# One core: a fixed TensorE order of four long runs per unit in place of planned, interleaved matmuls

## The chip, the cores and the metric

The kernel runs on one core of a Trainium2 chip. The metric is the device time of one execution in microseconds (us). Engine names as in the profile: PE is TensorE, PEld its weight loads, DVE is VectorE, ACT is ScalarE, POOL is GpSimd, SP is the engine that issues most DMAs.

## The reference

Three networks follow each other: windowed attention (4 batches, 8 heads, 576 positions), a gated feed-forward network on 2304 tokens of width 512, and a mixture over 8 experts, the "second network" here. Only the last is touched by the change:

```python
logits = x @ w_gate                          # 2304 x 8
P = np.exp(logits - logits.max())
for _ in range(8):                           # row and column scaling in turn
    P /= P.sum(1, keepdims=True) + 1e-09
    P /= P.sum(0, keepdims=True) + 1e-09
    P *= N / E
for e in range(8):
    h = np.maximum(x @ w1[e], 0.0)           # 2304 x 512 @ 512 x 1024
    out += P[:, e:e + 1] * (h @ w2[e])       # 2304 x 1024 @ 1024 x 512
```

## The kernel before

Every float32 operand is split into a high and a low part, and a product is made of three matmuls (high by high, high by low, low by high).

The second network is cut into 48 units: three groups of 768 tokens, and in each group 16 half experts (512 of an expert's 1024 hidden columns). Odd groups go through the half experts backwards, so the weights at a group's border are kept.

**First matrix of a unit, `gemm1`.** `x @ w1` is made with seven block products in place of eight (a Strassen-like scheme). The sums of weight blocks (s1 to s4) and of token blocks (t1 to t4) are formed ahead. A block product for one of two tiles q of 128 hidden columns is six matmuls of 384 columns (`product`, line 696). Each q has three PSUM banks, pa, pb and pc, and they are used several times in a unit: pa takes a11·b11, is copied by ACT (`p1`, line 720), takes s2·t2 on top, is copied again (`pq`, line 725), then s1·t1 (copied to `u4`, line 732) and at last s4·b22. pb takes s3·t3 and later a22·t4, but only after DVE has read it for the sum `u4` (line 733). pc takes a12·b21. Each of the four results is put through a relu by ACT (line 708) and split by DVE (line 709) into a tile `hh[u, f, t]`, with f from 0 to 3 the hidden tile and t the half of 384 tokens.

**Second matrix, `gemm2`.** For each of six tiles j of 128 tokens, twelve matmuls of 512 columns (line 753) go into one of two banks `py`, and DVE adds the result, scaled by P, to `acc[j]` (line 774; in a group's first half expert ACT writes it). j = 0 to 2 read the `hh` tiles with t = 0, j = 3 to 5 those with t = 1.

**Side work.** `moe2_weights` loads, sums and splits the next half expert (raw `w1r` and `st_w` by SP's DMAs, sums by POOL, high casts by ACT, low parts by DVE and POOL). `x_load` and `x_split` do the same for the next group's tokens. `side` is the routing: the last gating block `gate(5)` (four steps of DMA `sx`, cast, POOL subtraction at line 451 and two matmuls at line 454; all three tiles of a step share three slots of the pool `stg`), a maximum over partitions on POOL (line 662), and eight rounds of row and column scaling on DVE, each with one matmul with `ones` (line 680) for the column sums.

**Order.** The program text runs unit u's `gemm1` and lets `gemm2` of unit u - 1 and the side work advance at its `yield`s. On PE, ACT, DVE and POOL a planner, which simulates the kernel, then orders the instructions by readiness and priority; the text's order is only a priority. So PE's queue mixes the matmuls of lines 696 and 753 in pieces as small as one. Within an engine's queue the order is fixed once built.

Of the kernel before, what the change touches and what calls it, by code (L numbers as in the profile page):

```python
# [8 lines left out]
F32 = mybir.dt.float32  # L9
F32R = mybir.dt.float32r  # L10
AF = mybir.ActivationFunctionType
ALU = mybir.AluOpType
# [5 lines left out]
P = 128  # L18
# [14 lines left out]
def attention_moe_kernel(  # L33
# [14 lines left out]
    nc = tc.nc  # L48
# [361 lines left out]
    GT, TH = 768, 384  # L410
# [21 lines left out]
    def x_split(g):  # L432
        for m in ("b11", "t3", "t2", "b21", "t1", "t4", "b22"):
            for k in range(2):
                src = xsum[g, k][m]
                w = wr.tile([P, 2, 512], F32R, tag="w", name=f"x_{g}_{m}_{k}")
                nc.scalar.copy(w[:, 0, :TH], src)
                nc.vector.tensor_tensor(out=w[:, 1, :TH], in0=src, in1=w[:, 0, :TH].bitcast(F32), op=ALU.subtract)
                xc[m, k] = w
            yield  # L440
# [161 lines left out]
    def run(g):  # L602
        for _ in g:
            pass
# [45 lines left out]
    acp = ctx.enter_context(tc.tile_pool(name="acp", bufs=1, reuse_waits="tile"))  # L650
    rawp = ctx.enter_context(tc.tile_pool(name="rawp", bufs=2, reuse_waits="tile"))
# [40 lines left out]
    def product(ps, a, b, ch, q, first):  # L692
        k = 0
        for kt in range(2):
            for s, t in PASSES:
                nc.tensor.matmul(  # L696
                    ps[:, :TH],
                    lhsT=w1s[ch, a, kt][:, s, q * P : q * P + P],
                    rhs=xc[b, kt][:, t, :TH],
                    start=first and k == 0,  # L700
                    stop=k == 5,
                    skip_group_check=True,
                )
                k += 1
# [6 lines left out]
        )  # L711
        hh[u, f, t] = h

    def gemm1(u, ch):
        for q in range(2):
            pool, tag = ((ps_mm, "mm"), (ps_a, "a"))[q]
            pa, pb, pc = (pool.tile([P, 512], F32, tag=tag, name=f"p{n}_{u}_{q}") for n in "abc")
            p1, pq, u4 = (acp.tile([P, TH], F32, tag=n, name=f"{n}_{u}_{q}", bufs=2) for n in ("p1", "pq", "u4"))
            product(pa, "a11", "b11", ch, q, True)
            nc.scalar.copy(p1, pa[:, :TH])  # L720
            yield 0
            product(pb, "s3", "t3", ch, q, True)
            yield 1
            product(pa, "s2", "t2", ch, q, False)
            nc.scalar.copy(pq, pa[:, :TH])  # L725
            yield 0
            product(pc, "a12", "b21", ch, q, True)
            nc.vector.tensor_tensor(out=p1, in0=pc[:, :TH], in1=p1, op=ALU.add)
            relu_split(u, q, 0, p1)
            yield 1  # L730
            product(pa, "s1", "t1", ch, q, False)
            nc.scalar.copy(u4, pa[:, :TH])
            nc.vector.tensor_tensor(out=u4, in0=pb[:, :TH], in1=u4, op=ALU.add)
            relu_split(u, 2 + q, 1, u4)
            yield 1
            product(pb, "a22", "t4", ch, q, False)
            nc.vector.tensor_tensor(out=pq, in0=pb[:, :TH], in1=pq, op=ALU.add)  # L737
            relu_split(u, 2 + q, 0, pq)
            yield 0
            product(pa, "s4", "b22", ch, q, False)  # L740
            relu_split(u, q, 1, pa[:, :TH])
            yield 0

    def gemm2(u, g, i, ch, last):
        e = ch // 2
        for j in range(GT // P):
            tt = g * (GT // P) + j
            th, jj = divmod(j, TH // P)
            ps = ps_o.tile([P, 512], F32, tag="o", name=f"py_{u}_{j}")
            k = 0  # L750
            for f in range(4):
                for a, bb in PASSES:
                    nc.tensor.matmul(  # L753
                        ps,
                        lhsT=hh[u, f, th][:, a, jj * P : jj * P + P],
                        rhs=w2s[ch, f][:, bb, :],
                        start=k == 0,
                        stop=k == 11,
                    )
                    k += 1  # L760
            if i == 0:
                acc[j] = acp.tile([P, DM], F32, tag=f"acc{j}", name=f"acc_{tt}")
                if g == 0:
                    nc.scalar.copy(acc[j], ps)
                else:
                    nc.scalar.activation(acc[j], ps, AF.Copy, scale=Pm[:, tt, e : e + 1])
            elif g == 0 and i == 1:
                nc.vector.tensor_tensor(out=acc[j], in0=ps, in1=acc[j], op=ALU.add)
            else:
                if g == 0 and i == 2:  # L770
                    nc.gpsimd.tensor_scalar(
                        out=acc[j], in0=acc[j], scalar1=Pm[:, tt, 0:1], scalar2=1.0, op0=ALU.mult, op1=ALU.mult
                    )
                nc.vector.scalar_tensor_tensor(  # L774
                    out=acc[j], in0=ps, scalar=Pm[:, tt, e : e + 1], in1=acc[j], op0=ALU.mult, op1=ALU.add
                )
            if last:
                nc.sync.dma_start(out[tt * P : tt * P + P, :], acc[j])
            yield


    units = []
# [1 line left out]
        chs = list(range(16)) if g % 2 == 0 else list(range(15, -1, -1))  # L784
        units += [(g, i, ch) for i, ch in enumerate(chs)]
    sgen = side()
    for u in range(len(units) + 1):
        g2 = iter(())
        if u > 0:
            pg, pi, pch = units[u - 1]  # L790
            g2 = gemm2(u - 1, pg, pi, pch, pi == 15)
        if u == len(units):
            run(g2)
            break
        g, i, ch = units[u]
        if u == 3:
            run(sgen)
        others = [sgen] if u else []
        if u + 1 < len(units) and units[u + 1][2] != ch:
            others.append(moe2_weights(units[u + 1][2], rawp))  # L800
        if i == 15 and u + 1 < len(units):
            others.append(x_load(g + 1))
        if i == 0 and u > 0:
            xs = x_split(g)
            next(xs, None)
            for _ in g2:
                next(xs, None)
                next(xs, None)
            run(xs)

        def step():
            for o in others:
                next(o, None)

        for more in gemm1(u, ch):
            step()
            if more:
                next(g2, None)
                step()
        run(g2)  # L820
        for o in others:
            if o is not sgen:
                run(o)


# [83 lines left out]
```

## Time and profile before

| | us |
|---|---|
| three runs: median (lowest to highest) | 2155.91 (2154.08 to 2159.35) |
| profiled execution: its time | 2154.89 |
| profiled execution: span of the trace | 2153.1 |
| span in the second network's units, about | 619 to 2150 |

The span is the time from the first to the last instruction on record; some 1.8 us lie around it. A matmul's recorded length goes on after the next one has begun, since matmuls are pipelined; the distance between two starts is what counts. The view "chain in order of time" gives such distances, merged over neighbours that write the same kind of tile.

### The profile page before, as it was taken

How to read it: one execution, taken by the hardware profiler on the slowest of the kernel's cores; microseconds unless marked ns; L12 is line 12 of the kernel's file. 1: busy time of each engine (PE TensorE's matmuls, PEld its weight loads, DVE VectorE, ACT ScalarE, POOL GpSimd, SP SyncE). 2: the span in 40 equal slices, each digit the busy share in tenths (PEclk: the TensorE clock that was granted, in tenths of full speed). 3: DMA queues.
4: the chain of work that ended last, by engine and by line, in shares of the span. 5: the costliest groups of instructions: out<-in, count | busy, mean ns of one | idle time of the engine just before them, and what ended most of it. 6: DMA issues, size and time to landing. Idle time of an engine off the chain costs nothing.

```text
span 2153.1 us, 32685 instructions
## 1 busy us (share of the span) xinstructions
PE 2085.3 (97%) x12546; PEld 1901.9 (88%) x12546; DVE 1227.0 (57%) x2119; ACT 891.6 (41%) x1914; POOL 778.3 (36%) x853
## 2 busy tenths in 40 slices
PE   4799999999998999999999999999999999999999
PEld 3788999999988789899899989989998898999897
DVE  6987323323166766566656556665656566566553
ACT  4565443334245334334434443443434444434431
POOL 3765222112255424334413433433333333333320
PEclk8899999999999999999999999999999999999999
DMA  9233221202132212122212211221222122122110
GB/s 269 77 122 107 73 71 56 70 26 74 43 117 84 69 59 79 54 65 79 69 59 88 79 54 64 79 71 55 71 88 75 53 79 79 52 67 79 60 40 35
DMA packets 83388, 160.90 MB, mean 75 GB/s; under 512 B 10528, under 2 KB 18336, under 8 KB 83232
## 3 DMA queue, kind: packets, MB, share of 16 engines
q1 hardware_dynamic: 76128, 140.63, 20.6%
q10 hardware_dynamic: 7104, 18.19, 3.0%
q8 instruction: 98, 1.61, 0.3%
q14 instruction: 58, 0.48, 0.1%
HBM read 149.34 MB, written 9.44 MB: 74 GB/s over the span
## 4 chain that ended last, share of the span: by engine, by line
PE 87%; DVE 5%; DMA 3%; ACT 2%; issue 2%; POOL 1%; SPq 1%; ACTq 0%; POOLq 0%; DVEq 0%
PE py L753 37%; PE pa L696 18%; PE pb L696 9%; PE po L346 6%; PE pg L372 5%; PE pv L372 5%; PE pc L696 5%; PE psX L183 1%; PE psS L139 1%; DMA sd_v<-in_w_val 1%; DMA st_w<-in_w 0%; DMA vbd<-in_vt 0%; DVE w L505 0%; DVE m_o L270 0%; DMA first<-in_kt 0%
## 5 line engine op out<-in xcount | busy, mean ns | idle before, releaser
L753 PE MATMUL py<-w,h 128*128 128x512 f32 x3456 | 862.1, 393 | 0.6 <-DVE acc L774 0.6
L753 PEld LDWEIGHTS py<-w,h 128*128 128x128 f32 x3456 | 644.8, 188 | 118.7 <-DVE acc L774 1.0
L522 POOL TENSOR_TENSOR w<-st_w,w 128x512 fp32r<-128x512 f32 x184 | 242.2, 1335 | 347.5 <-ACT w L521 338.8
L774 DVE SCALAR_TENSOR_TENSOR acc<-py,Pm,acc 128x512 f32<-128x512 f32 x264 | 194.2, 748 | 277.9 <-PE py L753 277.3
L696 PE MATMUL pa<-x_b,w 128*128 128x384 f32 x1152 | 253.7, 337 | 7.9 <-ACT w L504 7.0
L491 POOL TENSOR_TENSOR w1s<-w1r 128x256 f32<-128x256 f32 x92 | 74.8, 813 | 505.3 <-DVE w L505 504.4
L696 PE MATMUL pa<-x_t,w 128*128 128x384 f32 x1152 | 244.9, 337 | 0.0
L696 PEld LDWEIGHTS pa<-x_b,w 128*128 128x128 f32 x1152 | 206.6, 188 | 19.3 <-ACT w L504 8.2
L696 PEld LDWEIGHTS pa<-x_t,w 128*128 128x128 f32 x1152 | 206.8, 188 | 14.5 <-ACT pq L725 0.3
L372 PE MATMUL pv<-xn,w_v 128*128 128x320 f32 (+1 forms) x1152 | 184.0, 302 | 7.2 <-ACT w_v L283 3.5
L521 ACT CAST w<-st_w 128x512 fp32r<-128x512 f32 x184 | 108.6, 621 | 186.6 <-PE pa L696 85.5
L346 PE MATMUL po<-h,w_o 128*128 128x320 f32 (+1 forms) x1152 | 179.1, 301 | 6.9 <-ACT partial L355 2.7
L372 PE MATMUL pg<-xn,w_g 128*128 128x320 f32 (+1 forms) x1152 | 182.5, 301 | 2.8 <-DVE hf L385 2.6
L372 PEld LDWEIGHTS pv<-xn,w_v 128*128 128x128 f32 x1152 | 164.8, 192 | 12.0 <-ACT w_v L283 4.1
L346 PEld LDWEIGHTS po<-h,w_o 128*128 128x128 f32 x1152 | 161.5, 190 | 12.6 <-DVE partial L357 3.5
L372 PEld LDWEIGHTS pg<-xn,w_g 128*128 128x128 f32 x1152 | 165.0, 193 | 7.1 <-DVE hf L385 3.4
L387 POOL TENSOR_TENSOR h<-hf,h 128x256 fp32r<-128x256 f32 (+1 forms) x96 | 80.7, 843 | 227.1 <-ACT h L386 227.1
L505 DVE TENSOR_TENSOR w<-w1s,w 128x512 fp32r<-128x512 f32 x184 | 124.5, 701 | 22.8 <-ACT w L504 20.6
L504 ACT CAST w<-w1s 128x512 fp32r<-128x512 f32 x184 | 111.3, 620 | 54.8 <-PE pc L696 17.7
L505 DVE TENSOR_TENSOR w<-w1r,w 128x512 fp32r<-128x512 f32 x92 | 110.5, 1201 | 36.6 <-ACT w L504 36.6
L708 ACT ACTIVATE h<-pq 128x384 fp32r<-128x384 f32 x96 | 50.3, 524 | 184.6 <-DVE pq L737 184.4
L696 PE MATMUL pb<-x_t,w 128*128 128x384 f32 x576 | 125.3, 336 | 0.0
(154 smaller groups left out, 2703.7 us busy)
## 6 DMA issues: line engine op xcount, KB each, us to landing
st_w<-in_w SPq DMA_DIRECT2D x184, 256.0 KB, 2.7
w1r<-in_w SPq DMA_DIRECT2D x184, 256.0 KB, 2.8
vbd<-in_vt ACTq DMA_DIRECT2D x30, 256.0 KB, 4.1
kbd<-in_kt ACTq DMA_DIRECT2D x30, 208.0 KB, 3.8
sd_g<-in_w_gate SPq DMA_DIRECT2D x10, 512.0 KB, 7.1
sx<-x2d SPq DMA_DIRECT2D x24, 192.0 KB, 2.4
xr<-x2d SPq DMA_DIRECT2D x12, 384.0 KB, 3.6
out<-acc SPq DMA_DIRECT2D x18, 256.0 KB, 2.1
```

Source lines behind the costliest of these rows:

```text
L346: nc.tensor.matmul(po[:, :n], lhsT=ow[f][:, a, dc * P : dc * P + P], rhs=hs[blk, f][:, bb, :n], start=k == 0, stop=k == 11,)
L372: nc.tensor.matmul(ps[:, :n], lhsT=w[kt, fg][:, a, fo * P : fo * P + P], rhs=xn[:, kt, bb, :n], start=k == 0, stop=k == 11,)
L387: nc.gpsimd.tensor_tensor(out=h[:, 1, :n], in0=hf, in1=h[:, 0, :n].bitcast(F32), op=ALU.subtract)
L491: nc.gpsimd.tensor_tensor(out=s1, in0=a21, in1=a22f, op=ALU.add)
L504: nc.scalar.copy(hi, src)
L505: nc.vector.tensor_tensor(out=lo, in0=src, in1=hi.bitcast(F32), op=ALU.subtract)
L521: nc.scalar.copy(w[:, 0, :], st)
L522: nc.gpsimd.tensor_tensor(out=w[:, 1, :], in0=st, in1=w[:, 0, :].bitcast(F32), op=ALU.subtract)
L696: nc.tensor.matmul(ps[:, :TH], lhsT=w1s[ch, a, kt][:, s, q * P : q * P + P], rhs=xc[b, kt][:, t, :TH], start=first and k == 0, stop=k == 5 ...
L708: nc.scalar.activation(h[:, 0, :], src, AF.Relu)
L753: nc.tensor.matmul(ps, lhsT=hh[u, f, th][:, a, jj * P : jj * P + P], rhs=w2s[ch, f][:, bb, :], start=k == 0, stop=k == 11,)
L774: nc.vector.scalar_tensor_tensor(out=acc[j], in0=ps, scalar=Pm[:, tt, e : e + 1], in1=acc[j], op0=ALU.mult, op1=ALU.add)
```

## The change

`gemm1` is cut into `gemm1_front` (the products a11·b11, s3·t3, s2·t2, a12·b21, s1·t1, each for both tiles q in turn: 60 matmuls of 384 columns) and `gemm1_back` (a22·t4 and s4·b22 for both q: 24 matmuls). `gemm2` is cut into halves of three token tiles (36 matmuls of 512 columns each). PE's instructions from the first unit on are put under `manual_schedule`, which keeps them in the text's order; the other engines are still ordered by the planner. The sequence of a unit u is: front of u, second half of `gemm2` of u - 1, back of u, first half of `gemm2` of u. At a group's first unit the second half of the unit before goes ahead of the front, and front and back follow each other directly. The side work moves one step after each block product and each token tile: 20 steps a unit. The matmuls of `gate(5)` and of the scaling rounds belong to the fixed order too: the gate's stand after the 2nd, 4th, 6th and 8th product of unit 1's front, the first scaling matmul after the first product of unit 1's back, the others three steps apart each. `x_split` begins in the first half of `gemm2` of a group's last unit, after `x_load` has been written out.

The instructions themselves (matmuls, copies, sums, DMAs) are the same in kind and number.

```diff
-    def gemm1(u, ch):
+    banks, snaps = {}, {}
+
+    def gemm1_front(u, ch):
         for q in range(2):
             pool, tag = ((ps_mm, "mm"), (ps_a, "a"))[q]
...
+        for q in range(2):
+            product(banks[q][0], "a11", "b11", ch, q, True)
+            nc.scalar.copy(snaps[q][0], banks[q][0][:, :TH])
+            yield
+        for q in range(2):
+            product(banks[q][1], "s3", "t3", ch, q, True)
+            yield
+        for q in range(2):
+            product(banks[q][0], "s2", "t2", ch, q, False)
+            nc.scalar.copy(snaps[q][1], banks[q][0][:, :TH])
+            yield
+        for q in range(2):
+            product(banks[q][2], "a12", "b21", ch, q, True)
+            p1 = snaps[q][0]
+            nc.vector.tensor_tensor(out=p1, in0=banks[q][2][:, :TH], in1=p1, op=ALU.add)
             relu_split(u, q, 0, p1)
-            yield 1
+            yield
+        for q in range(2):
+            pa, pb, _ = banks[q]
+            u4 = snaps[q][2]
             product(pa, "s1", "t1", ch, q, False)
             nc.scalar.copy(u4, pa[:, :TH])
             nc.vector.tensor_tensor(out=u4, in0=pb[:, :TH], in1=u4, op=ALU.add)
             relu_split(u, 2 + q, 1, u4)
-            yield 1
+            yield
+
+    def gemm1_back(u, ch):
+        for q in range(2):
+            pq, pb = snaps[q][1], banks[q][1]
             product(pb, "a22", "t4", ch, q, False)
             nc.vector.tensor_tensor(out=pq, in0=pb[:, :TH], in1=pq, op=ALU.add)
             relu_split(u, 2 + q, 0, pq)
-            yield 0
+            yield
+        for q in range(2):
+            pa = banks[q][0]
             product(pa, "s4", "b22", ch, q, False)
             relu_split(u, q, 1, pa[:, :TH])
-            yield 0
+            yield

-    def gemm2(u, g, i, ch, last):
+    def gemm2(u, half):
...
-        for j in range(GT // P):
+        for j in range(3 * half, 3 * half + 3):
...
-        for more in gemm1(u, ch):
-            step()
-            if more:
-                next(g2, None)
-                step()
-        run(g2)
...
+    order2 = ExitStack()
+    order2.enter_context(tc.manual_schedule(engines={mybir.EngineType.PE}))
+    for u, (g, i, ch) in enumerate(units):
+        others = [x for x in others if x is xs] if u and i == 0 else []
+        if i == 0 and u:
+            steps(gemm2(u - 1, 1))
+            run(xs)
+            others = []
+        if u:
+            others.append(sgen)
...
+        steps(gemm1_front(u, ch))
+        if i:
+            steps(gemm2(u - 1, 1))
+        steps(gemm1_back(u, ch))
+        if xl is not None:
+            run(xl)
+            xs = x_split(g + 1)
+            others.append(xs)
+        if u == 2:
+            run(sgen)
+        steps(gemm2(u, 0))
...
+    run(gemm2(len(units) - 1, 1))
+    order2.close()
```

Here `steps(g)` runs a generator and advances every entry of `others` once after each of its steps.

## Rows read from the trace of the kernel before

**Rows 1.** The page, parts 1 and 2: busy time, and granted clock in 40 slices.

```profile
PE 2085.3 (97%) x12546; PEld 1901.9 (88%) x12546; DVE 1227.0 (57%) x2119; ACT 891.6 (41%) x1914; POOL 778.3 (36%) x853
...
PEclk8899999999999999999999999999999999999999
```

**Rows 2.** The page, part 4: the chain that ended last, by line.

```profile
PE py L753 37%; PE pa L696 18%; PE pb L696 9%; PE po L346 6%; PE pg L372 5%; PE pv L372 5%; PE pc L696 5%; PE psX L183 1%; PE psS L139 1%; DMA sd_v<-in_w_val 1%; DMA st_w<-in_w 0%; DMA vbd<-in_vt 0%; DVE w L505 0%; DVE m_o L270 0%; DMA first<-in_kt 0%
```

**Rows 3.** Windows, all work: length, busy us and count per engine, clock, DMA.

```profile
618.90:745.00 126.10, 112.90 (x577) 101.20 (x576) 80.79 (x162) 56.13 (x119) 66.58 (x68) 0.97 0.28 90
760.00:2130.00 1370.00, 1370.00 (x6824) 1233.75 (x6823) 815.93 (x1232) 555.32 (x1140) 486.08 (x492) 1.00 0.21 67
```

**Rows 4.** Windows, line 753 alone: length, PE busy (count), weight loads (count), clock.

```profile
618.90:745.00 126.10, 39.98 (x153) 30.09 (x154) 0.97 0.28 90
760.00:2130.00 1370.00, 794.10 (x3189) 593.11 (x3188) 1.00 0.21 67
```

**Rows 5.** Windows, line 696 alone, same columns.

```profile
618.90:745.00 126.10, 69.25 (x360) 62.86 (x360) 0.97 0.28 90
760.00:2130.00 1370.00, 695.49 (x3635) 644.94 (x3635) 1.00 0.21 67
```

**Rows 6.** The chain in order of time, 1000 to 1040 us: start, us, what.

```profile
1002.50 0.70 PE py L753 x3
1003.19 1.06 PE pa L696 x6
1004.25 4.12 PE py L753 x18
...
1009.96 1.04 PE pb L696 x6
...
1012.56 2.08 PE py L753 x9
...
1022.49 5.48 PE py L753 x24
...
1029.90 2.76 PE py L753 x12
```

**Rows 7.** Waits of TensorE, 618.9 to 745 us: total, times, longest.

```profile
PE pa L696 <- ACT w L504: 7.0, 2, 4.0
PE pc L680 <- DVE csum L676: 3.1, 3, 2.0
PE pc L696 <- DVE h L709: 2.2, 2, 1.6
```

**Rows 8.** Timeline of TensorE, 680 to 700 us: start, us, what, idle before.

```profile
687.79 1.77 PE L696 MATMUL pa<-x_b,w 128*128 128x384 f32 x6 [3.98 <-ACT w L504]
...
689.64 4.07 PE L753 MATMUL py<-w,h 128*128 128x512 f32 x12
```

**Rows 9.** Timeline of GpSimd, 600 to 690 us.

```profile
665.91 1.01 POOL L451 TENSOR_TENSOR g<-sx,g 128x384 fp32r<-128x384 f32 x1
669.88 1.02 POOL L451 TENSOR_TENSOR g<-sx,g 128x384 fp32r<-128x384 f32 x1 [2.96 <-ACT g L450]
...
685.65 0.38 POOL L662 PARTITION_ALL_REDUCE gm<-gm  x1 [6.70 <-issue]
```

**Rows 10.** Timeline of VectorE, 676 to 742 us.

```profile
711.88 0.17 DVE L681 TENSOR_SCALAR csum<-pc 128x8 f32<-128x8 f32 x1 [0.48 <-PE pc L680]
...
713.85 0.42 DVE L676 TENSOR_REDUCE csum<-Pm 128x8 f32<-128x144 f32 x1
```

**Rows 11.** Groups of VectorE: count, busy us, mean ns, idle before by releaser.

```profile
L774 DVE SCALAR_TENSOR_TENSOR acc<-py,Pm,acc 128x512 f32<-128x512 f32 x264 | 194.2, 748 | 277.9 <-PE py L753 277.3
...
L709 DVE SCALAR_TENSOR_TENSOR h<-pq,h 128x384 fp32r<-128x384 f32 x96 | 71.1, 741 | 27.0 <-ACT h L708 27.0
...
L737 DVE TENSOR_TENSOR pq<-pb,pq 128x384 f32<-128x384 f32 x96 | 52.9, 551 | 32.4 <-PE pb L696 32.3
```

**Rows 12.** The page, part 5: one group of ScalarE.

```profile
L708 ACT ACTIVATE h<-pq 128x384 fp32r<-128x384 f32 x96 | 50.3, 524 | 184.6 <-DVE pq L737 184.4
```

More of the change, by code (lines that the diff above doesn't have):

```diff
@@ L712, in relu_split @@
         hh[u, f, t] = h
-    def gemm1(u, ch):
+    banks, snaps = {}, {}
+    def gemm1_front(u, ch):
         for q in range(2):
             pool, tag = ((ps_mm, "mm"), (ps_a, "a"))[q]
[L717 to L720, printed above, removed]
-            yield 0
-            product(pb, "s3", "t3", ch, q, True)
-            yield 1
-            product(pa, "s2", "t2", ch, q, False)
-            nc.scalar.copy(pq, pa[:, :TH])
-            yield 0
-            product(pc, "a12", "b21", ch, q, True)
-            nc.vector.tensor_tensor(out=p1, in0=pc[:, :TH], in1=p1, op=ALU.add)
+            banks[q] = [pool.tile([P, 512], F32, tag=tag, name=f"p{n}_{u}_{q}") for n in "abc"]
+            snaps[q] = [acp.tile([P, TH], F32, tag=n, name=f"{n}_{u}_{q}", bufs=2) for n in ("p1", "pq", "u4")]
+        for q in range(2):
[13 more added lines that the diff above has]
+            nc.vector.tensor_tensor(out=p1, in0=banks[q][2][:, :TH], in1=p1, op=ALU.add)
             relu_split(u, q, 0, p1)
-            yield 1
+            yield
+        for q in range(2):
+            pa, pb, _ = banks[q]
+            u4 = snaps[q][2]
             product(pa, "s1", "t1", ch, q, False)
@@ L734, in gemm1 @@
             relu_split(u, 2 + q, 1, u4)
-            yield 1
+            yield
+    def gemm1_back(u, ch):
+        for q in range(2):
+            pq, pb = snaps[q][1], banks[q][1]
             product(pb, "a22", "t4", ch, q, False)
@@ L738, in gemm1 @@
             relu_split(u, 2 + q, 0, pq)
-            yield 0
+            yield
+        for q in range(2):
+            pa = banks[q][0]
             product(pa, "s4", "b22", ch, q, False)
             relu_split(u, q, 1, pa[:, :TH])
-            yield 0
-    def gemm2(u, g, i, ch, last):
+            yield
+    def gemm2(u, half):
+        g, i, ch = units[u]
+        last = i == 15
         e = ch // 2
-        for j in range(GT // P):
+        for j in range(3 * half, 3 * half + 3):
             tt = g * (GT // P) + j
@@ L786, in attention_moe_kernel, with steps @@
     sgen = side()
[L787 to L792, printed above, removed]
-            run(g2)
[L794 to L798, printed above, removed]
+    others = []
+    def steps(g):
+        for _ in g:
+            for o in others:
+                next(o, None)
+    order2 = ExitStack()
[5 more added lines that the diff above has]
+            run(xs)
+            others = []
+        if u:
+            others.append(sgen)
         if u + 1 < len(units) and units[u + 1][2] != ch:
             others.append(moe2_weights(units[u + 1][2], rawp))
+        xl = None
         if i == 15 and u + 1 < len(units):
[L802 to L813, printed above, removed]
-        for more in gemm1(u, ch):
-            step()
-            if more:
-                next(g2, None)
-                step()
-        run(g2)
+            xl = x_load(g + 1)
+            others.append(xl)
+        steps(gemm1_front(u, ch))
[9 more added lines that the diff above has]
+        steps(gemm2(u, 0))
         for o in others:
-            if o is not sgen:
+            if o is not sgen and (xl is None or o is not xs):
                 run(o)
+    run(gemm2(len(units) - 1, 1))
+    order2.close()
 def _layout(inputs):
```

## The prediction

> **What bounds the kernel now.** I began with the page's busy times: PE is busy in 97% of the span, no other engine in more than 57%, and the granted clock is at its upper level of 2.4 GHz in nearly all slices [rows 1]. The chain that ended last runs along PE, and the two lines that the change reorders, 753 and 696, make up more than two thirds of it [rows 2]. So only PE's own stream counts, and an edit of its order can act in two ways: by idle time and by the distance between matmuls.
>
> Idle time next. The windows show two different stretches. From 760 to 2130 us PE is busy in all 1370.00 us [rows 3]: 44 units without a wait. From 618.9 to 745 us, where the second network begins, it is busy in 112.9 of 126.1 us, with a clock of 0.97 [rows 3], and the waits say for what: 7.0 us for a weight cast of ACT, 3.1 us for the column sums of the scaling, 2.2 us for a relu's low part [rows 7]. There is nothing to win from waits in the steady stretch, and something to lose.
>
> Then the distances. A long run of line 753 shows them by subtraction [rows 6]: 9 matmuls take 2.08 us, 12 take 2.76, 18 take 4.12 and 24 take 5.48. From the ninth on each adds 0.2267 us (2.72 us for the last twelve of 24), but the first nine take 0.231 each: 0.04 us more than nine at the later pace. Line 696 does the same. The six of pa at 1003.19 us, right behind three of py, take 1.06 us, and the six of pb at 1009.96 us, which stand behind others of line 696, take 1.04, or 0.1733 each. So each change from one kind to the other costs some 0.02 us into line 696 and 0.04 us into line 753, paid in the first matmuls behind the change.
>
> How much does the steady stretch pay? 3189 matmuls at 0.2267 are 722.9 us [rows 4], 3635 at 0.1733 are 630.0 us [rows 5]; together 1352.9 of 1370 us. 17.1 us, or 0.39 us a unit (6824 matmuls are 43.7 units of 156), are what the mixing costs. A unit takes 31.32 us now and would take 30.88 without any change of kind.
>
> The Trainium skill, "TensorE: Matmul & The Clock Gate", section "Back-to-back issue gap", gives the distance of isolated matmuls at full clock as columns / 2.4 plus 2.5 ns, with no term for the matmul before. Rows 6 disagree with that form: equal matmuls of 512 columns stand 0.231 or 0.2267 us apart by their place in a run. By the Trainium skill the new order would gain nothing in the steady stretch; by the rows it gains most of 17 us. That is rival E below.
>
> **The change part by part.** *Long runs.* Two runs of each kind a unit pay 2 x (0.02 + 0.04) = 0.12 us, where 0.39 is paid now: 0.27 us less. For the 46 units behind 745 us this is 12.5 us. Bounds: nothing, if the extra is not due to the change of kind; 18 us (46 x 0.39), if long runs shed all of it. I take 12.5, since four rows of rows 6 agree on it to a hundredth.
>
> *Fixed order in the steady stretch.* PE now waits where before it had other matmuls in its queue. Four places could be late, and I hold each against its slack:
> - The third token tile of a half needs the bank of the first, 2.76 us after that ended; DVE's sum takes 0.75 [rows 11]. Slack 2.0 us.
> - The first token tile of the first half needs, at its tenth matmul, the `hh` tile of the last a22·t4. Between them stand two products (2.08 us) and nine matmuls (2.08). The way is a DVE sum of 0.55, a relu of 0.52 and a DVE split of 0.74 [rows 11, 12], with handovers some 2.2 us. Slack 2.0 us.
> - s2·t2 and s1·t1 go on top of pa after an ACT copy, with three products (3.1 us) since the product copied. Slack about 2.5 us.
> - a22·t4 needs pb read by DVE; half a `gemm2` (8.2 us) covers that, except at a group's first unit, where one product (1.04 us) stands in for it, against a copy and a sum of about 1.3 us with handovers. That is 0.3 us at least, up to 2 if DVE is at other work: three times, 1.5 us together.
> DVE is busy in 60% of this stretch, ACT in 41% [rows 3], and each works in its own order, so two or three instructions ahead can use up 2 us. Nearest row: the waits of today, none in 1370 us. Below: 0. Above: 0.6 us a unit. I take 1.5 us in all, near the row of today.
>
> *The start, 619 to 745 us.* Now: 360 products' matmuls are 62.4 us and 153 of line 753 34.7 [rows 4, 5]; the 64 others [rows 3] are at most 11 us at a product's pace and nearer 7. So 18 to 22 us are lost, of which 12.3 are waits [rows 7]; the rest is clock and changes of kind (behind the wait of 3.98 us twelve of line 753 are drawn 4.07 us long, against 2.76 [rows 6, 8]). I take 20. Under the fixed order:
> - The gate's matmuls stand two products (2.08 us) apart, and the chain of a step (DMA, cast, POOL) repeats at 4.0 us at best, from one POOL subtraction at 665.91 us to the next at 669.88, as its three tiles fill the three slots [rows 9]. PE did other work meanwhile; now it waits 1.5 us for each of three steps at least, and twice that when POOL or SP are busy with weights, plus up to 4 for the first. Taken 8 (5 to 13).
> - The maximum over partitions arrives after 6.7 us of POOL idling to its issue [rows 9]; three token tiles and a product (9.2 us) stand before the first scaling matmul, against about 11 us with one pass on DVE. Taken 2 (0 to 5).
> - A scaling pass on DVE lasts from 711.88 to 714.27 us, 2.4 us, with the matmul about 2.9 [rows 10]. Four of the rounds have only three products, 3.1 us, between their matmuls. Alone that suffices; with DVE busy in 64% of the stretch [rows 3] other work slips in. Taken 1.5 us for each of four, 6 (0 to 14).
> - Unit 0: the second unit's weights are wanted 8.2 us later than now, so of the 7.0 us [rows 7] I keep 3, as ACT's copies can still stand behind a cast that waits for its DMA. Clock lost behind all these waits: 2.
> Sum 21 against 20 now: plus 1 us, between minus 11 and plus 17.
>
> *Side work.* 20 steps a unit, as DVE's and POOL's instructions are the same; their load hides under PE (60% and 35% of 1370 us [rows 3]). Cost nothing; without that cover they would show as waits of line 696 for casts. The six token tiles at a group's border (16.4 us) cover `x_split` as they do now. The queue of SP is not reordered by hand.
>
> *Sum.* -12.5 + 1.5 (borders) + 1.5 + 1 = -8.5 us on the profiled execution's 2154.9: 2146.4. That execution lies 1.0 us below the median of the runs shown, so I say **2147 us**.
>
> **The rivals.** Measurement tells about 0.3%, 6.5 us, from no change.
> - A, as summed: 2142 to 2149, chance 0.42.
> - B, the start gets cheaper too, because PE no longer needs unit 1's weights early and the planner sets DVE's order to PE's: 12.5 and 5 more off, about 2138. For it: 7.0 us waited for casts [rows 7]. Against: the gate's steps in PE's fixed order. 0.10.
> - C, the start eats the gain: gate 13, maximum 5, scaling 10 and 5 for the rest are 33 against 20, and with the 3 us of borders and slack that makes 2156 to 2159. For it: the 4.0 us step and DVE's 64%. 0.22.
> - D, slower: the `hh` tile of the last a22·t4 comes late in every unit, since DVE has weight splits queued before it. From 0.27 us a unit the gain is gone, from 0.41 on it is slower by 0.3%; with 0.6 us, 27.6 us are paid for 12.5, about 2171. For it: ACT's relus idled 184.4 us for that very DVE sum [rows 12], and DVE's splits 27.0 us for ACT [rows 11]. Against: the slack of 2.0 us. 0.18.
> - E, the extra does not hang on the change of kind (it comes with other traffic, say) and stays: 2160 by the other terms, or 2155 with a kinder start. Against: the same pattern in four runs [rows 6]. 0.08.
>
> **How the numbers follow.** Faster by more than 0.3%: B and nearly all of A, 0.50. Within 0.3%: C, most of E and A's upper edge, 0.30. Slower: D and the rest of E, 0.20. The range for 8 in 10 reaches from B's 2138 through C to the mild half of D: 2138 to 2163. Faster alone would be 2136 to 2149.
>
> **What would show it.** In the profile after: the steady stretch at about 31.0 us a unit, runs of 24, 36 and 60, 36 of line 753 in 8.2 us; L454 and L680 behind waits of POOL and DVE between 650 and 720 us; the end of that start no more than a few us from where it is now. Wrong would be: distances of 0.231 us through a whole run (E), or waits of line 753 for line 709, or of pa for line 725, spread over all units (D), or idle time of more than 30 us before unit 3 (C).

## The result, and the profile after

The changed kernel takes 2174.45 us (median of four runs, 2172.61 to 2176.27), the kernel before on the same chip 2155.95 (four runs, 2154.08 to 2159.35). The ratio is 1.0086, 95% interval 1.0074 to 1.0098: slower, above the range of the forecast. The profiled execution took 2173.12 us, its span is 2171.3.

The first look goes to the busy times and the clock, as in [rows 1]:

```profile
PE 2084.4 (96%) x12546; PEld 1906.0 (88%) x12546; DVE 1207.3 (56%) x2119; ACT 891.2 (41%) x1914; POOL 810.0 (37%) x853
...
PEclk7899999999998999999999999999999999999999
```

PE is busy for 0.9 us less than before, and the span is 18.2 us longer: on balance the time went into idle time of PE (the long runs shorten its busy time, and matmuls at the lower clock, below, lengthen it). The windows say where (columns as in [rows 3]):

```profile
618.90:745.00 126.10, 103.28 (x503) 91.53 (x502) 76.16 (x156) 50.96 (x105) 61.69 (x61) 0.92 0.27 83
760.00:1100.00 340.00, 340.00 (x1712) 308.45 (x1711) 199.90 (x307) 138.53 (x285) 135.85 (x132) 1.00 0.22 69
1146.00:1180.00 34.00, 31.04 (x147) 27.49 (x148) 19.84 (x31) 10.70 (x23) 13.08 (x12) 0.95 0.33 108
```

From 760 to 1100 us, within a group, there is no wait, as forecast. The start has 9.6 us less busy time than in [rows 3], at a clock of 0.92 instead of 0.97, and at a group's border (1146 to 1180) there are now waits.

The pace within a group is seen in the chain in order of time, same stretch as [rows 6] (line 776 is line 753 of before):

```profile
1005.28 8.20 PE py L776 x36
1013.49 2.10 PE pb L696 x12
1015.59 2.08 PE pa L696 x12
1017.67 8.20 PE py L776 x36
1025.87 2.10 PE pa L696 x12
```

The first twelve behind a change of kind take 2.10 us, the twelve behind them 2.08, and 36 of line 776 take 8.20 (36 x 0.2267 + 0.04). A front, 2.10 and four times 2.08, takes 10.43 us by its starts (1025.87 to 1036.30 in the same view), so a unit is 10.43 + 8.20 + 4.18 + 8.20 = 31.01 us; 31.00 was forecast.

To compare kernels I use one number that needs no windows: **PE's loss**, the time since the first matmul of line 696 minus 0.1733 us for each 384-column matmul of line 696 and 0.2267 us for each matmul of line 753 or 776 that has been started (the steady paces of [rows 6]). Read at marks of such work done (the second network has 1482 us of it), it splits the difference. 400 to 540 and 900 to 1060 are the stretches of work that hold the two borders.

| loss in us | to 100 | 100 to 400 | 400 to 540 | 540 to 900 | 900 to 1060 | to the end | whole |
|---|---|---|---|---|---|---|---|
| before | 29.1 | 4.3 | 1.8 | 4.4 | 2.0 | 6.1 | 47.6 |
| after | 39.8 | 1.3 | 8.2 | 1.6 | 9.9 | 1.8 | 62.6 |

The start costs 10.7 us more. The borders cost 15.4 more than the 2.7 us that the long runs alone would leave in them (that is what e2, below, shows). The rest costs 11.2 less. That is 14.9. The remaining 3.3 us of the 18.2 lie ahead of the first such matmul, which starts at 622.4 us instead of 619.1. This looks like scatter between executions: the work ahead of it is the same 4997 matmuls in all kernels of this study, and in their profiled executions the first of line 696 starts between 618.6 and 623.2 us; a copy of the kernel before with one POOL instruction replaced (e10) had 622.3.

The waits of TensorE after, 615 to 760 us, and then 760 to 2130 us ([rows 7] answer to the first):

```profile
PE pc L680 <- DVE csum L676: 12.2, 4, 8.3
PE pb L696 <- DVE u L746: 5.9, 1, 5.9
PE pl L454 <- ACT g L450: 1.5, 2, 1.0
PE pl L454 <- POOL g L451: 1.5, 2, 0.7
```

```profile
PE py L776 <- DVE h L709: 5.1, 2, 2.5
PE pb L696 <- DVE u L746: 3.8, 2, 1.9
PE py L776 <- ACT h L708: 1.3, 2, 0.7
```

Each line of the second list stands for two waits, one at each border. Neither list has the casts of ACT that led [rows 7]: those 7.0 us are gone, and others have come.

**A border.** The timeline of TensorE after, around the first border (the six tiles; of the next unit's front and back only the wait between them):

```profile
1141.56 1.55 PE L776 MATMUL py<-w,h 128*128 128x512 f32 x6
1143.78 0.73 PE L776 MATMUL py<-w,h 128*128 128x512 f32 x2 [0.67 <-ACT h L708]
1147.05 16.49 PE L776 MATMUL py<-w,h 128*128 128x512 f32 x64 [2.54 <-DVE h L709]
...
1175.88 2.38 PE L696 MATMUL pb<-x_t,w_a 128*128 128x384 f32 x12 [1.91 <-DVE u L746]
```

From the ninth matmul on, line 776 wants the low parts (line 709) of this unit's a22·t4. The queues of ACT and then of DVE show what stands ahead of them:

```profile
1142.38 0.92 ACT L437 CAST x_b<-xr 128x384 fp32r<-128x384 f32 x2
1143.21 0.94 ACT L708 ACTIVATE h<-pq 128x384 fp32r<-128x384 f32 x2
```

```profile
1141.50 0.55 DVE L755 TENSOR_TENSOR pq<-pb,pq 128x384 f32<-128x384 f32 x1
1141.97 0.55 DVE L438 TENSOR_TENSOR x_b<-xr,x_b 128x384 fp32r<-128x384 f32 x1
1142.43 1.95 DVE L438 TENSOR_TENSOR x_t<-xt,x_t 128x384 fp32r<-128x384 f32 x4
1144.31 1.28 DVE L505 TENSOR_TENSOR w<-w1s,w 128x512 fp32r<-128x512 f32 x2
1145.51 1.02 DVE L438 TENSOR_TENSOR x_b<-xr,x_b 128x384 fp32r<-128x384 f32 x2
1146.45 1.02 DVE L709 SCALAR_TENSOR_TENSOR h<-pq,h 128x384 fp32r<-128x384 f32 x2
...
1172.49 2.87 DVE L709 SCALAR_TENSOR_TENSOR h<-p,h 128x384 fp32r<-128x384 f32 x2
```

The second of the two sums `pq` is ready at 1142.05 and ACT's relus of both start at 1143.21, behind casts of the next group's tokens (line 437). On DVE the splits of these tokens (line 438) and of weights (line 505) go first, and the relus' splits start at 1146.45. The tokens are that late because their second half waits for PE on POOL:

```profile
1136.26 1.30 POOL L426 TENSOR_TENSOR xt<-xr,xr 128x384 f32<-128x384 f32 x1 [23.96 <-PE py L776]
```

Its tiles come free only near the end of the run of line 776 that began at 1129.18 us. Before, POOL waited 23.16 us at the same place, and PE had other matmuls to do meanwhile. In a fixed order it has none.

**The start.** Timeline of TensorE after (the two longest waits, and a run behind them):

```profile
644.97 4.21 PE L696 MATMUL pb<-x_t,w_a 128*128 128x384 f32 x12 [5.88 <-DVE u L746]
...
700.61 0.57 PE L680 MATMUL pc<-csum,ones 128*128 128x8 f32 x2 [8.25 <-DVE csum L676]
701.02 10.21 PE L776 MATMUL py<-w,h 128*128 128x512 f32 x36
```

Of the 10.7 us more, 8.4 are listed waits (21.5 in the view above with two more lines of 0.2 each, 13.1 in the same view of before; line 346, of the network ahead, is left out). The rest lies behind them: twelve matmuls of pb take 4.21 us instead of 2.27, 36 of line 776 are drawn 10.21 us long instead of 8.36. The granted clock is 0.50, the lower level of 1.2 GHz, from 644.97 to 648.98 us, and 0.81 on average from 701.02 to 711.08. The wait of 8.25 us goes back over three engines, POOL, ACT and DVE:

```profile
684.35 0.38 POOL L662 PARTITION_ALL_REDUCE gm<-gm  x1 [5.91 <-PE py L776]
691.75 0.72 POOL L494 TENSOR_TENSOR w1s<-w1r,w1s 128x256 f32<-128x256 f32 x1 [7.02 <-issue]
```

```profile
692.50 0.62 ACT L504 CAST w<-w1s 128x512 fp32r<-128x512 f32 x1 [3.30 <-POOL w1s L494]
```

```profile
690.36 0.30 DVE L683 SCALAR_TENSOR_TENSOR Pm<-Pm,csum 128x144 f32<-128x144 f32 x1
693.15 1.10 DVE L505 TENSOR_TENSOR w<-w1s,w 128x512 fp32r<-128x512 f32 x1 [2.48 <-ACT w L504]
...
695.71 0.29 DVE L670 TENSOR_REDUCE rsum<-Pm 128x18 f32<-128x144 f32 x1
...
700.05 0.41 DVE L676 TENSOR_REDUCE csum<-Pm 128x8 f32<-128x144 f32 x1
```

POOL stands for 7 us behind the maximum, so a weight sum, its cast and its split are late, and the scaling's next steps stand behind that split on DVE, and behind further splits of weights and relus up to 699.3 us. From the last step of one round to the column sums of the next it takes 10.1 us here, for a pass that took 2.4 in all in [rows 10].

### The profile page after: what moved, and what is told of

The parts are those of the page before. It is cut to its first block, busy times and chain, and to the rows that moved or that the text cites. A ratio compares the mean times of both kernels' runs of the same rounds, so it can differ in the third digit from the quotient of the medians.

```text
span 2171.3 us, 32703 instructions
## 1 busy us (share of the span) xinstructions
PE 2084.4 (96%) x12546; PEld 1906.0 (88%) x12546; DVE 1207.3 (56%) x2119; ACT 891.2 (41%) x1914; POOL 810.0 (37%) x853
## 3 DMA queue, kind: packets, MB, share of 16 engines
q1 hardware_dynamic: 76128, 140.63, 20.9%
## 4 chain that ended last, share of the span: by engine, by line
PE 85%; DVE 4%; issue 1%; DMA 1%; POOL 1%; ACT 1%; ACTq 0%; POOLq 0%; DVEq 0%
PE py L776 36%; PE pa L696 18%; PE pb L696 9%; PE po L346 5%; PE pv L372 5%; PE pg L372 5%; PE pc L696 4%; PE psS L139 1%; DMA sx<-x2d 1%; PE psX L183 1%; DVE x_t L438 1%; DVE w L505 0%; DVE h L709 0%; PE psXT L223 0%; PE pl L454 0%
## 5 line engine op out<-in xcount | busy, mean ns | idle before, releaser
L776 PE MATMUL py<-w,h 128*128 128x512 f32 x3456 | 809.2, 392 | 6.7 <-DVE h L709 5.1
L491 POOL TENSOR_TENSOR w1s<-w1r 128x256 f32<-128x256 f32 x92 | 93.1, 1012 | 754.6 <-DVE w L505 754.6
L522 POOL TENSOR_TENSOR w<-st_w,w 128x512 fp32r<-128x512 f32 x184 | 252.4, 1383 | 70.1 <-ACT w L521 70.1
L738 DVE TENSOR_TENSOR p<-pc,p 128x384 f32<-128x384 f32 x96 | 53.6, 558 | 337.0 <-PE pc L696 335.6
L696 PE MATMUL pa<-x_b,w 128*128 128x384 f32 x1152 | 219.2, 338 | 0.0
L696 PE MATMUL pa<-x_t,w 128*128 128x384 f32 x1152 | 215.7, 334 | 0.2 <-ACT pq L733 0.2
L726 ACT COPY p<-pa 128x384 f32<-128x384 f32 x96 | 46.1, 481 | 384.4 <-PE pa L696 384.4
L696 PEld LDWEIGHTS pa<-x_t,w 128*128 128x128 f32 x1152 | 201.0, 188 | 0.6 <-ACT pq L733 0.6
L521 ACT CAST w<-st_w 128x512 fp32r<-128x512 f32 x184 | 114.1, 623 | 165.5 <-PE py L776 157.3
L696 PE MATMUL pb<-x_t,w_a 128*128 128x384 f32 x576 | 112.7, 345 | 9.7 <-DVE u L746 9.7
```

What stands on the lines that cost most here:

```text
L491: nc.gpsimd.tensor_tensor(out=s1, in0=a21, in1=a22f, op=ALU.add)
L521: nc.scalar.copy(w[:, 0, :], st)
L522: nc.gpsimd.tensor_tensor(out=w[:, 1, :], in0=st, in1=w[:, 0, :].bitcast(F32), op=ALU.subtract)
L696: nc.tensor.matmul(ps[:, :TH], lhsT=w1s[ch, a, kt][:, s, q * P : q * P + P], rhs=xc[b, kt][:, t, :TH], start=first and k == 0, stop=k == 5 ...
L738: nc.vector.tensor_tensor(out=p1, in0=banks[q][2][:, :TH], in1=p1, op=ALU.add)
L776: nc.tensor.matmul(ps, lhsT=hh[u, f, th][:, a, jj * P : jj * P + P], rhs=w2s[ch, f][:, bb, :], start=k == 0, stop=k == 11,)
```

## Experiments

Times are medians, ratios go to the runs of the kernel before on the same chip. In these sets the kernel before had medians from 2154.5 to 2158.2 us, so a difference of medians between two rows can be off by 3 to 4 us; the loss columns come from one profiled execution each. The table holds all fifteen; the texts follow.

| kernel | us | ratio, 95% interval | loss to 100 | borders | whole |
|---|---|---|---|---|---|
| e1 fixed order from unit 3 on | 2173.14 | 1.0075, 1.0053 to 1.0096 | 40.6 | 9.4 + 8.0 | 62.4 |
| e2 planner at the borders | 2156.03 | 0.9996, 0.9986 to 1.0005 | 39.5 | 1.3 + 1.4 | 46.6 |
| e3 no maximum | 2165.19 | 1.0037, 1.0024 to 1.005 | 31.4 | 9.3 + 9.1 | 54.4 |
| e4 tokens staged | 2166.77 | 1.0044, 1.003 to 1.0057 | 40.5 | 5.7 + 5.7 | 56.3 |
| e5 border as a unit | 2160.82 | 1.0029, 1.0018 to 1.004 | 40.3 | 4.2 + 3.8 | 52.7 |
| e6 old start | 2165.89 | 1.0046, 1.0029 to 1.0064 | 35.4 | 8.2 + 9.5 | 57.5 |
| e7 = e6 + e2 | 2151.24 | 0.998, 0.997 to 0.9989 | 33.2 | 1.3 + 2.1 | 41.3 |
| e8 short runs | 2246.49 | 1.0424, 1.0403 to 1.0444 | 39.7 | | 137.0 |
| e9 fixed order from unit 1 on | 2172.61 | 1.0075, 1.0057 to 1.0092 | 38.2 | 9.8 + 8.3 | 60.7 |
| e10 before, no maximum | 2148.7 | 0.9953, 0.9939 to 0.9966 | 20.9 | 1.8 + 2.0 | 39.5 |
| e11 short runs, covered | 2219.04 | 1.0278, 1.0264 to 1.0292 | 38.7 | | 106.2 |
| e12 = e7, old start to unit 3 | 2146.19 | 0.9942, 0.9929 to 0.9954 | 29.4 | 1.3 + 1.4 | 36.8 |
| e13 P half a unit later | 2154.32 | 0.9997, 0.9987 to 1.0006 | 39.6 | 1.3 + 1.4 | 46.7 |
| e14 = e13, fixed from unit 3 | 2156.84 | 1.0011, 1.0002 to 1.0021 | 40.6 | 1.3 + 1.4 | 47.7 |
| e15 = e13, fixed from unit 4 | 2148.96 | 0.9976, 0.9967 to 0.9985 | 33.1 | 1.7 + 1.4 | 40.7 |

### Start or borders: e1, e2, e9

```diff
 # e1 (e9: u == 1)
-    order2.enter_context(tc.manual_schedule(engines={mybir.EngineType.PE}))
     for u, (g, i, ch) in enumerate(units):
+        if u == 3:
+            order2.enter_context(tc.manual_schedule(engines={mybir.EngineType.PE}))
 # e2
         steps(gemm1_back(u, ch))
+        if i == 0 and u:
+            order2.enter_context(tc.manual_schedule(engines={mybir.EngineType.PE}))
         if xl is not None:
+            order2.close()
             run(xl)
```

> The fixed order starts with unit 3; in units 0 to 2 PE is ordered by the planner, the text as in the changed kernel. Theory S (the start loses because PE is bound to the text's order there: of the 18.2 us between the two profiled executions, 10.7 us are lost between the first product and 100 us of PE work): about 8 to 11 us faster than the changed kernel, 2164 to 2167 us; the waits of 5.9 us (pb for the sum u) and 8.3 us (second scaling matmul) gone or below 4. Rival R (the start is late because POOL, ACT and DVE are late there whatever PE does): within 3 us of the changed kernel, 2172 to 2177.

> The fixed order is lifted from the first half of the second product of a group's last unit to the end of the next unit's back, twice in the kernel; all else as changed. Theory B (each border loses 8.3 us because PE must wait there for relus that stand behind the next group's splits on ACT and DVE): 10 to 16 us faster than the changed kernel, 2159 to 2164. Rival C (the splits are simply too much work in that stretch for DVE and ACT): at most 4 us faster, 2170 or more.

> The changed kernel with unit 0 left to the planner, fixed order from unit 1. Theory U (of the 10.7 us that the start loses more than before, some 6 are unit 0's: a22t4 directly behind s1t1, with ACT's copies and DVE's sum behind weight casts): loss before 15 us of PE work 7 to 9 us in place of 14.7, 5 to 8 us faster than the changed kernel, 2167 to 2170. Rival (the weights of unit 1 are late anyway and the wait only moves): within 3 us, 2172 or more.

e2 gives back 18.4 us by the medians (some 16 of the loss), more than theory B's 10 to 16, so the borders are the larger part of the miss. The only wait of its whole stretch from 760 to 2130 us is this one:

```profile
PE py L776 <- DVE h L709: 0.2, 1, 0.2
```

The splits do not come sooner in e2. Its timelines at the first border, DVE and then TensorE:

```profile
1145.98 1.01 DVE L709 SCALAR_TENSOR_TENSOR h<-pq,h 128x384 fp32r<-128x384 f32 x2
```

```profile
1144.04 1.23 PE L696 MATMUL pb<-x_t,w 128*128 128x384 f32 x6
```

On DVE the token and weight splits still stand ahead of the relus' splits, which start at 1145.98 (1146.45 in the kernel after). What changed is that PE does matmuls of the next unit's front in that time. No run kept PE's fixed order and put the relus' splits first on ACT and DVE.

e1 and e9 give back next to nothing at the start (loss to 100 of 40.6 and 38.2 for 39.8), as their rivals said. In e1 the loss at 60 us of work falls from 35.8 to 16.4, but at 80 it is 35.5: PE comes sooner to the scaling matmuls and stands there. e9 moves unit 0's wait in the same way (loss at 15 us of work 7.7 against 14.7, at 30 16.2 against 17.9).

### What the border waits for: e4, e5

e4 loads the second half of the tokens into the weights' staging tiles, which no unit uses at that time, so that it need not wait for tiles of weights that the second product still reads. e5 puts a group's first unit in the order of all others as well (second half of `gemm2` between front and back) and runs `x_split` out ahead.

```diff
 # e4, in x_load
+            if g and k:
+                raw = [rawp.tile([P, 2, 512], F32, tag="raw", name=f"xr_{g}_{k}_{i}") for i in range(2)]
...
+                t.append(rawp.tile([P, 2, 512], F32, tag="sums", name=f"xt_{g}_{k}_1", bufs=1))
 # e5, besides
-        if i == 0 and u:
-            steps(gemm2(u - 1, 1))
-            run(xs)
...
-        if i:
+        if u:
             steps(gemm2(u - 1, 1))
...
-            if o is not sgen and (xl is None or o is not xs):
+            if o is not sgen:
                 run(o)
```

> At a border the second half of the next group's tokens is loaded into the weights' staging tiles, which no unit uses then, in place of slots that come free only when the second product of the unit before has ended; order and work as changed. Theory B1 (the splits bunch in front of the relus because their inputs come some 25 us late): POOL's 24 us wait for line 776 goes, the waits of PE for relus at 1143 and 1147 us too, and with them the half clock; 8 to 13 us faster, 2162 to 2167, with about 2 us left per border for pb. Rival C (too much split work, whenever its inputs come): the same waits, within 4 us of the changed kernel.

> All in the fixed order, with the staged tokens of the run before, and a border treated as any other unit: first half, front of the next group's first unit, second half, back, so that 8.2 us of the second product stand between s1t1 and a22t4. Theory B2 (what was left per border with staged tokens, some 5 us, is the wait for pb of 1.9 us, splits in front of relus and the clock behind these): at least the wait for pb goes, 3 to 9 us off the staged kernel's 2166.8, 2158 to 2164. Rival (the splits now have only 8.2 us of cover and hold up the front's first product): waits of pa for x splits of 2 us or more per border, 2166 or slower.

e4 gives back 7.7 us, e5 13.6 in all (6.3 and 9.9 of the loss). The waits of e4 from 760 to 2130 us (its lines stand five lower, 701 for 696 and so on):

```profile
PE pb L701 <- DVE u L751: 3.8, 2, 1.9
PE py L781 <- DVE h L714: 2.0, 2, 1.0
PE py L781 <- DVE acc L802: 1.7, 2, 0.9
```

In e5 the first of them is gone and the others are nearly as here. So the late tokens made the wait for line 709 longer (the longest was 2.5 us, and is 1.0 in e4), and the direct step from front to back made the one for `u`. Some 5 us at both borders together are left in e5 (8.0 against the 2.7 of e2, in which PE's order is free there).

### What slows the start: e3, e10, then e6, e7, e12

e3 and e10 replace the maximum over partitions by a constant, in the kernel after and in the one before; e6, e7 and e12 give the first units the text of before.

```diff
 # e3, e10
-        nc.gpsimd.partition_all_reduce(gm[:, 1:2], gm[:, 0:1], P, bass_isa.ReduceOp.max)
+        nc.gpsimd.memset(gm[:, 1:2], 0.0)
 # e6 (old_unit: text and side work of before; order2 opens behind run(sgen), and unit 3 makes
 # all six tiles of unit 2 behind its front; e12: u < 4, order2 opens at u == 4)
+        if u < 3:
+            old_unit(u, ch)
+            continue
+        if u == 3:
+            run(sgen)
```

> The maximum over partitions on POOL is left out (0 is subtracted in its place); all else as changed. Theory P (POOL stands still for 6 to 7 us before and again 7 us after that instruction, and a weight sum behind it holds up ACT, DVE and with them the second scaling matmul): the waits of 1.9 and 8.3 us of PE for the column sums fall below 3 in all, the clock drop behind them goes too, 9 to 13 us faster than the changed kernel, 2161 to 2166. Rival Q (the scaling passes are slow because DVE has other work in its queue): the wait of 8.3 us stays above 4, 2 to 5 us faster.

> The kernel before without the maximum over partitions (0 is subtracted in its place), a control for the 8.4 us that the changed kernel won by the same cut. Theory P1 (the free order of before hides most of POOL's standstill): 1 to 4 us faster than before. Rival P2 (the standstill costs both kernels alike): 7 to 10 us faster than before, and then it is no part of what the change cost.

> Units 0 to 2 in the text and order of the kernel before, fixed order from unit 3, borders as in the changed kernel; unit 3 makes all six token tiles of unit 2 between its front and its back. Theory S2 (the start loses because the changed text wants P in unit 2's first half already, and because front and back of unit 0 follow each other directly; freeing PE alone could not mend that): the loss before 100 us of PE work falls from 39.8 to about 29 us, 9 to 11 us faster than the changed kernel, 2163 to 2166. Rival R2 (the start is late for POOL's maximum and the late weights, whatever the text): within 4 us of the changed kernel, 2170 or more.

> The start as before, the fixed order from unit 3 on but lifted at the two borders. If the three terms add up (start 10 us back, borders 16 us back, long runs 12 us kept): 2144 to 2148 against about 2156 before, 0.4 to 0.6% faster than before. If they do not add up (the planner puts the loss elsewhere): 2152 to 2157.

> As the run of 2151.2 us, but units 0 to 3 in the old text and order, so that the last scaling rounds still have unit 3's work to hide behind; fixed order from unit 4, lifted at the borders. If the 4 us that that run lost more than before between 60 and 100 us of PE work were the fixed order's: 2146 to 2149, 0.3 to 0.5% faster than before. If they come with the late P whatever stands there: 2150 to 2152.

Without the maximum the kernel after gains 9.3 us and the kernel before 9.5 (some 8 of the loss each). The maximum, with the standstill of POOL around it, costs both alike, so it is no part of the change's price, although the longest wait of after leads to it. It is also not all of that wait: e3 has theory P's time, but PE still waits 6.8 us for the column sums, at most 4.7 at once, where P said below 3 in all and rival Q (DVE's other work) above 4 for the longest. The old start gives back 4.4 us of loss in e6, 6.3 in e7 against e2, and 10.1 in e12: there the start loses what it lost before (29.4 against 29.1), and the kernel is faster than both, 0.58% below before. e6 came in at theory S2's time but not at its loss (35.4 for 29), e7 between its two forecasts, e12 where the fixed order's theory put it.

### Which part of the start: e13, e14, e15

On top of e2, the first half of `gemm2` of unit 2 goes into unit 3, behind its front, so that P is wanted later; e14 and e15 also leave PE to the planner until unit 3 or 4.

```diff
         steps(gemm1_front(u, ch))
+        if u == 3:
+            run(sgen)
+            steps(gemm2(u - 1, 0))
...
-        if u == 2:
-            run(sgen)
-        steps(gemm2(u, 0))
+        if u != 2:
+            steps(gemm2(u, 0))
```

> Base: e2, the fixed order lifted at the two borders, 2156.0 us. One thing is moved: the first half of gemm2 of unit 2 goes from the end of unit 2 into unit 3, behind its front, and the side work is run out right before it instead of before the end of unit 2. So the scaling factors P are wanted one front (about 10 us) later and the last scaling rounds have more of PE's work between them; the text, the fixed order and the gate's places in units 0 and 1 stay. Theory S (the start's extra 10.7 us come from P being wanted half a unit earlier): PE's loss before 100 us of its own work falls from 39.5 us to 30 to 35, and the time to 2147 to 2152. Rival G (the loss comes from the fixed places of the gate's and the scaling's matmuls and from late weights, and moves on to the next wait): within 2.5 us of 2156.

> Base: e13 (borders lifted, first half of gemm2 of unit 2 in unit 3 behind its front; 2154.3 us, 39.6 us lost before 100 us of PE work). One thing is added: PE's order is fixed from unit 3 on only, so the planner orders units 0 to 2, as in e1. Theory J (two things bind together: PE's fixed order makes it stand at the scaling's matmuls, and P wanted in unit 2 leaves the planner nothing to put into the gap; each alone, e1 and e13, gives nothing back): the loss falls to 29 to 35 us, the time to 2144 to 2150. Rival T (the new text's order of the start is worse in itself, since DVE's and ACT's order follows it): within 3 us of 2154, the loss 37 or more.

> As e14, with PE's order fixed from unit 4 on, so that unit 3, into which the scaling's end and the moved half fall, is ordered by the planner too. Theory J: the loss of 100 us of PE work near that of before and e12 (29 us), the time 2143 to 2149. Rival T: within 3 us of 2154.

e13 gives nothing back: theory S falls, PE stands at the same scaling matmuls. e14 misses theory J's numbers too, and meets rival T's. Timelines of TensorE, e14 and then e15, around the fourth and fifth scaling matmuls:

```profile
721.74 0.28 PE L680 MATMUL pc<-csum,ones 128*128 128x8 f32 x2
727.48 0.60 PE L680 MATMUL pc<-csum,ones 128*128 128x8 f32 x2 [5.46 <-DVE csum L676]
730.55 0.60 PE L680 MATMUL pc<-csum,ones 128*128 128x8 f32 x2 [2.47 <-DVE csum L676]
```

```profile
721.02 1.20 PE L696 MATMUL pb<-x_t,w_a 128*128 128x384 f32 x6
...
727.09 0.28 PE L680 MATMUL pc<-csum,ones 128*128 128x8 f32 x2
...
730.78 0.39 PE L680 MATMUL pc<-csum,ones 128*128 128x8 f32 x2 [2.07 <-DVE csum L676]
```

In e14 unit 3's front is done at 721.74, and its back, which needs no P, stands in the fixed order behind the scaling matmuls and the tiles of line 776 (it begins at 762.21). In e15 the planner takes that back (pb<-x_t,w_a at 721.02) and the first products of unit 4 ahead. e15 is 7.9 us faster than e14 on the same chip, with 7.5 us less loss to 100 (5.4 us and 6.5 of that loss against e13). So with P wanted later, PE's freedom through unit 3 gives most of the start's price back. Later P alone gives nothing (e13), and neither does freedom that ends before unit 3, with P early (e1) or late (e14). e15 with P at its old place was not run, so it is not shown that later P is needed. e15 reaches theory J's time but not its loss (33.1 for 29), and the 3.7 us of loss to 100 between e15 and e12 are open.

### Is it the length of the runs: e8, e11

Both start from e2 and spread the three tiles of the second half over the front, from a group's fifth unit on: after the 3rd, 6th and 9th product (e8) or the 2nd, 6th and 10th (e11).

```diff
+            for n in (2, 4, 4):      # e8: (3, 3, 3)
+                for _ in range(n):
+                    next(front)
+                next(tiles)
+            run(front)
```

> The kernel with the order lifted at the borders (2156.0 us), but in 36 of the 48 units the three token tiles of the second half stand between groups of three products: four runs of each kind a unit in place of two. Theory L (each change of kind costs 0.02 us into line 696 and 0.04 us into line 776 in the first matmuls behind it): 36 x 2 x 0.06 = 4.3 us slower, 2160.3, and a unit of 31.13 us in place of 31.01. Rival E (the extra distance in the kernel before came from other traffic): same unit time, 2156. Rival W (shorter runs cost by waits for banks or relus): over 8 us slower, with waits in the steady units.

> The kernel with the order lifted at the borders (2156.0 us), in 36 units the token tiles of the second half behind the 2nd, 6th and 10th product of the front: four runs of each kind a unit, as in the run of 2246 us, but with a token tile left between s1t1 and a22t4. Theory L (a change of kind costs 0.06 us a pair): 4.3 us slower than 2156.0, a unit of 31.13 us, no waits. Rival E (length of run does not matter): 2156, 31.01 us. Theory W (the 2.9 us a unit of the earlier run came from taking the cover away, not from short runs) is held by either; if the units again take over 33 us, W falls.

Both lose far more than changes of kind cost: e8 as its rival W said, with waits spread over the units, and e11 unlike all its forecasts of time. A unit takes some 32.93 us in e11 (1006.67 to 1039.60 below). Its timelines of TensorE and then VectorE:

```profile
1006.67 2.27 PE L696 MATMUL pa<-x_b,w 128*128 128x384 f32 x12
...
1029.61 2.97 PE L776 MATMUL py<-w,h 128*128 128x512 f32 x11
1033.80 5.97 PE L776 MATMUL py<-w,h 128*128 128x512 f32 x25 [1.22 <-DVE h L709]
1039.60 2.27 PE L696 MATMUL pa<-x_b,w 128*128 128x384 f32 x12
```

```profile
1031.49 1.78 DVE L505 TENSOR_TENSOR w<-w1s,w 128x512 fp32r<-128x512 f32 x1
1033.20 0.55 DVE L709 SCALAR_TENSOR_TENSOR h<-pq,h 128x384 fp32r<-128x384 f32 x1
```

The half with the wait takes 9.99 us (1029.61 to 1039.60) instead of 8.20. The rest is 32.93 - 1.79 = 31.14 us: two more pairs of changes at 0.06 us on the 31.01 of after make 31.13. So the price per change holds, and the wait behind the weight split (line 505) is the prediction's rival D, at the place that it named. In the kernel after the same relu split ends at 1049.92 us (line 709 from 1048.36 for 1.56 us), some 1.1 us before the matmul that wants it, the twelfth of the run that starts at 1048.52: with a run of 36 between front and back it is in time.

## Why the prediction was wrong

- **Long runs.** Right: 31.01 us a unit for 31.00 forecast, 0.27 us less per unit than before, as reckoned (2.9 against 8.7 us of loss in the 660 us of work from 100 to 400 and 540 to 900, or 21.4 units); 11.2 us outside the start for a term of 12.5. Rival E is out. (The 31.32 us given for a unit of before do not fit the sum: 30.88 + 0.39 is 31.27; the window held somewhat more of line 753 than whole units do. The forecast does not use it.)
- **The step that failed: "The six token tiles at a group's border (16.4 us) cover `x_split` as they do now", and with it the 1.5 us for the three places behind a group's first front.** The borders cost 15.4 us. In a fixed order the tiles are no cover at the point where it counts, since they are the ones that wait: they need the unit's own relu splits, and these stand behind the next group's casts and splits on ACT and DVE. In e2 the queue of DVE is as late, and PE, free to take the next front, loses nothing. I counted the cover's length and did not ask what the cover itself needs. The direct step to the back waits 1.91 us at each border, within the bound of 2; in unit 0 it waits 5.88, beyond it.
- **The start.** Mis-sized: +10.7 us for +1, within the bounds of -11 and +17. The gate's waits were 3.0 us (8 taken), those for the weights' casts none (3 kept), those for the column sums 12.2 (8 taken for maximum and scaling), and unit 0's pb 5.9. That freeing PE in the first units alone would mend it was my next theory, and e1 and e9 refute it; e15 gives the larger part back with P wanted later and PE free through unit 3, and whether both are needed is open.
- **Slack in the steady stretch.** Right: no wait from 760 to 1100 us, though the slack for the last a22·t4, taken as 2.0 us, is some 1.1. Rival D's mechanism exists (e11), not in this order.
- **Rival C** (the start eats the gain) happened in size, and in part by other places: the gate took 3.0 us of waits and not 13, and the listed waits are 21.5 us, below the 30 that were to be its sign. Without the border its time would have been the result, as e2 at 0.9996 shows.

## What to carry to other kernels

Fixing an engine's order paid here where the work repeats, and cost where something irregular passes through (a group's border, a serial chain that starts late): try to fix the repeating part and leave the rest to the planner, as e12 does. When a stretch of work is named as cover for late data, look at what that stretch itself waits for, and at which queue stands ahead of it on every engine it passes. A wait that vanishes in an experiment is worth something only if the loss some units later has fallen too; read the loss at several marks.

## What the runs showed of the hardware

- The price of a change between the two kinds of matmul holds to a hundredth of a us: 2.10 us for the first twelve 384-column matmuls behind 512-column ones, 2.08 for later ones, 8.20 us for 36 of 512. The two kinds differ in column count, operands and banks; which of these sets the price was not tested.
- Behind a partition maximum recorded as 0.38 us POOL starts nothing for 7.02 us, and it stood 6.70 ahead of it in [rows 9]; the two kernels lose 9.3 and 9.5 us to the maximum (e3, e10).
- One DVE relu split takes 0.55 us in most places of these timelines, but two took 2.87 us at 1172.49, while POOL ran line 522 from 1172.11 to 1174.95. In the trace of after from 760 us on, none of the 71 splits of line 709 with no POOL instruction beside them took over 0.56 us, and all 81 that took over 0.9 had one; many short ones had one too. No run tested this.
- A wait of PE costs more than it lists: at the first border 5.1 us are listed, and 6.9 are lost beyond the 1.3 of the long runs. Most of the rest is the clock: granted 0.50 from 1148.55 to 1151.96 us, within the 64 matmuls of line 776 that take 16.49 us; at the steady pace they would be drawn some 14.7 us long.
